# Attention with a mixture-of-experts step on one core: q, k and v loaded as one transfer of 128 partitions each

## The chip, the cores and the metric

One core of a Trainium2 chip. The metric is device time in microseconds of one execution of the whole program; what the host does before the launch (laying out arrays) is not in it.

## The reference

q, k and v have 8 batches, 8 heads, 576 positions and 64 columns of float32. Per batch and head: q and k are rotated by position, the scores are `q_rot @ k_rot.T / 8`, a softmax follows over the keys, and the result is `attn @ v`. The heads of a batch are put beside each other into x (8, 576, 512). Then, per batch:

```python
scores = np.einsum('bsd,d->bs', x, w_gate)
top_idx = np.argpartition(-scores[b], capacity)[:capacity]   # capacity = 128
xe = x[b, top_idx]
ye = np.maximum(xe @ w1, 0.0) @ w2                           # 512 -> 1024 -> 512
g = 1.0 / (1.0 + np.exp(-scores[b, top_idx]))
out[b, top_idx] = x[b, top_idx] + g[:, None] * ye
```

## The kernel before

The work goes in 32 **pairs** of heads (`n_pairs = B * NP`, four to a batch). Of a pair, 512 of the 576 positions lie as 128 partitions with 4 positions each, the other 64 apart. A pair passes these steps:

- **load** (line 388): k into `k_in`, q into `q_in`, v into `vt`, two buffers each, for the pair after next. k takes 2 transfers, q 3 and v 6, all issued on SyncE's queue (SP) by `dma` (L398). `vt` holds v twice, in partitions 0 to 63 and again in 64 to 127; this comes from a broadcast in the transfer: the source has a leading dimension of 2 with a step of zero.
- **rotate** (L434): on GpSimd, for pair 0 on VectorE; scratch tile `m`. **turn_qk** (L496 to L520): TensorE transposes, and ScalarE, VectorE and GpSimd split the result into a high and a low part (kh, kl, qh, ql).
- **attend**: nine units of 128 queries by 576 keys. Units 0 to 7 go in twos on the halves of TensorE (L588), unit 8 alone; VectorE finds each row's maximum (L605), ScalarE makes exponentials into `pab` (L609), and VectorE transposes these in blocks of 32 into `pt` (L623). Units 0 to 3 go into `pt0`, called c = 0, units 4 to 8 into `pt1`, c = 1. There is one buffer of each.
- **move** (L636): the 32-wide blocks have to change partitions, which is done by six transfers from SBUF to SBUF per c, on SP's queue too. Four can go at once, the last two wait for the first two:

```python
gone = [part(g, 2, g + 1, 0, turns) for g in (0, 2)]
for i, g in enumerate((0, 2)):
    part(g + 1, 2, g + 1, 1, turns)
for i, g in enumerate((0, 2)):
    part(g + 1, 0, g, 1, turns + [gone[i]])
```

- **value** (L665): 36 matmuls of TensorE per c (72 instructions in the profile), pt against v; for c = 0 they are all 64x128, for c = 1 some are 64x192. Copies to `ot` (L298, L300), transposes and gate scores (L709, L710), and rows times the softmax's reciprocals into `x` (L720) follow; each half batch is stored by two transfers (L772, L774).
- **route** and **experts** (L792 to L969), once per batch, are spread between the pairs that follow. w1 and w2 are loaded once, early (L995).

The order on each engine is not that of the code. Every step is recorded as an `Op` with engines, a key (a due time), the operations that it waits for and two durations: how long it holds its engine, and when its result is there. `Order.run` places them all by list scheduling and then emits them in that order. For transfers these pairs of numbers are constants: `LOAD, STORE = {"SP": (500, 2900)}, {"SP": (650, 4000)}` and `(700, 3300)` for a move. A transfer's size doesn't enter.

Of the kernel before, what the change touches and what calls it, by code (L numbers as in the profile page):

```python
# [227 lines left out]
def attention_moe_kernel(ctx: ExitStack, tc: tile.TileContext, q, k, v, w_gate, w1, w2, rope, outs, cap):  # L228
# [159 lines left out]
    def load(pi, names="kqv", after=()):  # L388
        b, j = divmod(pi, NP)
        key = at(pi, 0) - KEY["load"]  # L390
        main = lambda src: src[b, 2 * j:2 * j + 2, 0:512, :].rearrange("h (p t) d -> p h t d", t=NT)
# [5 lines left out]
        def dma(n, dst, src, use, late):  # L397
            o = op(LOAD, lambda: nc.sync.dma_start(dst, src), key + late, use.before + list(after))  # L398
            use.by(o)
            got[n].append(o)  # L400

        for n, src, use, late in (("k", k, kin, 0), ("q", q, qin, 1)):
            if n not in names:
                continue
            dst = use.tile
            dma(n, dst[:, 0:2 * NT, :].rearrange("p (h t) d -> p h t d", h=2), main(src), use, late)
            if n == "k":
                dma(n, dst[0:REM, 2 * NT:NS, :], src[b, 2 * j:2 * j + 2, 512:S, :].rearrange("h p d -> p h d"), use, late)
            else:
# [568 lines left out]
    def weights():  # L978
# [7 lines left out]
        for h in range(2):  # L986
            const_ready.append(op(LOAD, lambda h=h: nc.sync.dma_start(
                wg[64 * h:64 * h + 64, :, h], w_gate.rearrange("(j h d) -> h d j", h=2, d=D)[h]),
                at(0, 0.1), anchors[-1:]))
# [63 lines left out]

# [21 lines left out]
```

## Time and profile before

| | |
|---|---|
| median of 3 runs | 1051.77 us (1051.35 to 1051.9) |
| the profiled execution | 1053.8 us; span from its first to its last instruction 1052.1 us |
| mean granted TensorE clock | 0.803 of full speed |
| busy share: TensorE, VectorE, ScalarE, GpSimd | 60%, 52%, 34%, 40% |
| SP's DMA queue (q1) | 83104 packets, 115.12 MB, 41.7% of 16 DMA engines |

The span is what the profile's rows are cut from; the profiled execution's own time is 1.7 us longer. No engine is busy for much more than half of it, so what the engines wait for has to be read from the waits, by group of instructions, and then in one pair. A name such as `ps<-pt,vt` says that tile ps was written from pt and vt. "PEld" is TensorE's loading of weights. In a line of waits, `<-` names what ended the wait. SP issues transfers; a row "SPq" shows how long its queue was taken by the issue, not how long the transfer ran.

### The profile page before, as it was taken

What the parts mean: (1) busy time and instruction counts of PE and PEld (TensorE: products, weight loads), DVE (VectorE), ACT (ScalarE), POOL (GpSimd) and SP (SyncE); (2) the same over time, 40 slices, a digit from 0 to 9 for tenths busy, and PEclk for the clock granted to TensorE, in tenths of its full rate; (3) what the DMA queues carried; (4) which work ended last, traced back from release to release, by engine and by line L of the source; (5) the groups of instructions that cost most, each with busy time, mean ns of one, the idle gap of its engine ahead of it and who ended that gap; (6) DMA issues with size and microseconds to landing.
All of it is one profiled execution on the core that took longest, in us unless ns stands there. A gap on an engine that the chain in (4) does not pass through costs nothing.

```text
span 1052.1 us, 20374 instructions
## 1 busy us (share of the span) xinstructions
PE 628.9 (60%) x7696; PEld 533.8 (51%) x7696; DVE 544.1 (52%) x1342; ACT 362.6 (34%) x967; POOL 422.7 (40%) x491
## 2 busy tenths in 40 slices
PE   5436544576555555766456874555765475676677
PEld 3325534465454444655345764444655464565565
DVE  7245333675445545545457553446553465664452
ACT  3235333453323334423234432323442333442221
POOL 2649355745424175144270534440643262500011
PEclk9977766787778888878778886778887788887899
DMA  3643655434553443445343354543345354234520
GB/s 93 161 117 110 173 147 133 104 96 131 127 144 99 131 115 88 127 106 148 101 120 96 89 164 102 148 116 101 99 110 147 91 137 113 75 93 104 131 86 31
DMA packets 84626, 121.11 MB, mean 115 GB/s; under 512 B 27056, under 2 KB 69040, under 8 KB 84528
## 3 DMA queue, kind: packets, MB, share of 16 engines
q1 hardware_dynamic: 83104, 115.12, 41.7%
q0 software_dynamic: 1280, 4.20, 1.3%
q8 instruction: 61, 1.00, 0.4%
q10 hardware_dynamic: 144, 0.49, 0.1%
q14 instruction: 37, 0.30, 0.1%
HBM read 44.53 MB, written 11.53 MB: 53 GB/s over the span
## 4 chain that ended last, share of the span: by engine, by line
PE 35%; DMA 22%; SPq 19%; DVE 8%; issue 6%; POOL 5%; ACT 4%; POOLq 0%; ACTq 0%; DVEq 0%
PE ps L665 20%; DMA pt<-pt 18%; SPq L398 12%; PE ps L588 6%; SPq L636 6%; DVE pt L623 4%; PE ps L930 3%; ACT pab L609 3%; DVE nm L605 3%; PE ps L709 2%; PE ps L496 2%; DMA k_in<-k_dram 2%; POOL m L434 1%; PE ps L710 1%; DMA vt<-v_dram 1%
## 5 line engine op out<-in xcount | busy, mean ns | idle before, releaser
L665 PE MATMUL ps<-pt,vt 64*64 64x128 f32 (+1 forms) x4608 | 244.5, 359 | 341.2 <-DMA pt<-pt 287.3
L665 PEld LDWEIGHTS ps<-pt,vt 64*64 64x64 f32 x4608 | 215.8, 176 | 364.9 <-issue 350.5
L623 DVE STREAM_TRANSPOSE pt<-pab 128x576 f32<-128x576 f32 x256 | 185.0, 752 | 358.8 <-PE ps L665 329.9
L609 ACT ACTIVATE pab<-ps,nm 128x576 f32<-128x576 f32 x256 | 187.5, 740 | 130.7 <-DVE nm L605 130.6
L605 DVE TENSOR_REDUCE nm<-ps 128x1 f32<-128x576 f32 x288 | 200.8, 733 | 25.1 <-PE ps L588 23.6
L298 ACT COPY ot<-ps 64x64 f32<-64x64 f32 (+1 forms) x124 | 32.2, 287 | 400.3 <-PE ps L665 399.3
L434 POOL TENSOR_TENSOR rk<-k_in,m 128x512 f32<-128x512 f32 (+1 forms) x62 | 52.7, 867 | 175.6 <-PE ps L496 175.0
L588 PE MATMUL ps<-kh,qh 64*128 64x288 f32 (+1 forms) x576 | 96.3, 359 | 17.2 <-ACT pab L609 9.3
L511 POOL TENSOR_TENSOR kl<-xf,kh 128x512 fp32r<-128x512 f32 x31 | 39.4, 1270 | 161.4 <-ACT xf L509 161.2
L588 PEld LDWEIGHTS ps<-kh,qh 64*128 64x128 f32 (+1 forms) x576 | 57.5, 201 | 46.6 <-issue 20.7
L588 PE MATMUL ps<-kh,ql 64*128 64x288 f32 (+1 forms) x576 | 75.8, 306 | 5.6 <-POOL ql L511 5.6
L588 PE MATMUL ps<-kl,qh 64*128 64x288 f32 (+1 forms) x576 | 76.1, 305 | 0.0
L434 POOL TENSOR_TENSOR rq<-q_in,m 64x64 f32<-64x64 f32 (+1 forms) x93 | 57.4, 632 | 43.6 <-PE ps L496 30.8
L434 POOL TENSOR_TENSOR m<-k_in,tabs 128x320 f32<-128x320 f32 x62 | 52.3, 860 | 36.4 <-DMA k_in<-k_dram 34.8
L709 PE MATMUL ps<-ident,ot 128*128 128x128 f32 x160 | 47.7, 311 | 26.5 <-ACT pab L609 25.1
L588 PEld LDWEIGHTS ps<-kh,ql 64*128 64x128 f32 (+1 forms) x576 | 58.1, 198 | 6.7 <-POOL ql L511 6.6
L588 PEld LDWEIGHTS ps<-kl,qh 64*128 64x128 f32 (+1 forms) x576 | 59.1, 199 | 0.0
L609 ACT ACTIVATION_READ_ACCUMULATOR pab<-ps,nm 128x1 f32 x256 | 51.2, 200 | 0.0
L930 PE MATMUL ps<-w,xt 128*128 128x512 f32 x192 | 51.2, 406 | 0.0
L930 PE MATMUL ps<-w,ht 128*128 128x512 f32 x192 | 51.1, 405 | 0.0
L710 PEld LDWEIGHTS ps<-wg,ot 128*128 128x128 f32 x320 | 49.7, 211 | 0.9
L511 POOL TENSOR_TENSOR ql<-xf,qh 128x512 fp32r<-128x512 f32 x31 | 39.4, 1270 | 26.0 <-ACT xf L509 26.0
(105 smaller groups left out, 860.1 us busy)
## 6 DMA issues: line engine op xcount, KB each, us to landing
pt<-pt SPq DMA_DIRECT2D x192, 180.0 KB
pt<-pt SPq DMA_DIRECT2D x192, 144.0 KB
vt<-v_dram SPq DMA_DIRECT2D x128, 128.0 KB
k_in<-k_dram SPq DMA_DIRECT2D x32, 256.0 KB
q_in<-q_dram SPq DMA_DIRECT2D x32, 256.0 KB
out_dram<-x SPq DMA_DIRECT2D x16, 512.0 KB
vt<-v_dram SPq DMA_DIRECT2D x64, 32.0 KB
xe<-w_dram SPq DMA_DIRECT2D x8, 256.0 KB
```

Of the source, the lines that this page charges most:

```text
L398: o = op(LOAD, lambda: nc.sync.dma_start(dst, src), key + late, use.before + list(after))
L434: lambda: e.tensor_tensor(out, in0, in1, op=alu), key, after)
L511: d = op({"POOL": pool(n)}, lambda: nc.gpsimd.tensor_tensor(lo, xf.tile, hi.bitcast(F32), op=ALU.subtract), key, [c, y] + lu.before)
L588: nc.tensor.matmul(bank_of(bs[i])[:, n, 0:HALF], lt, rt, start=first, stop=last)
L605: lambda: nc.vector.tensor_reduce(nm.tile[:, u:u + 1], bank_of(b)[:, :, 0:HALF], axis=AX.XY, op=ALU.max, negate=True),
L609: lambda: nc.scalar.activation(dst.rearrange("p (n c) -> p n c", n=2), bank_of(b)[:, :, 0:HALF], AF.Exp, bias=nm.tile[:, u:u + 1], scale=1 ...
L623: lambda: nc.vector.transpose(pt[c].tile[:, 0:2, :, to, :].rearrange("p w m j -> p m w j"), src.rearrange("p (m w j) -> p m w j", w=2, j=32)),
L636: lambda: nc.sync.dma_start(flat[32 * to:32 * to + 32, w_to], flat[32 * at_:32 * at_ + 32, w_at]),
L665: nc.tensor.matmul(bank_of(acc)[64 * h:64 * h + 64, g, :].rearrange("p (w c) -> p w c", w=2)[:, :, c0:c0 + n], vt.tile[gp_, h, m % 2 * NT ...
L709: nc.tensor.transpose(bank_of(b)[:, i * P:i * P + P], cols, ident)
L710: nc.tensor.matmul(bank_of(b)[:, 400 + 2 * i:402 + 2 * i], cols, wg[:, j, :], start=True, stop=True)
L930: nc.tensor.matmul(bank_of(bank), lhs.tile[:, a, c * P:c * P + P], w[w_][:, c, fs], start=(c == 0 and i == 0), stop=(c == n - 1 and i == 2))
```

## The change

k, q and v come from the host in the layout that they have in SBUF, and each pair's load of each is one transfer with 128 rows: 640, 576 and 1152 elements a row. The host fills the rows that k leaves out of its last two blocks with zeros (which replaces a memset of `k_in`), writes v twice, and lays out the gate's vector in the same manner (two transfers and a memset become one transfer). `Order.run` gets a second clock for SP, `moving`: a transfer's data take 3.6 ns per KB, one after the other, and the result is there a constant time after that. The constants of loads, stores and moves change with it. The size of all three loads is given as 320.

```diff
+    PER_KB = 3.6
...
+                    if e == "SP":
+                        moving = max(moving, begin + takes) + self.PER_KB * o.size
+                        begin += max(0.0, moving - begin - takes)
...
-                    free[e] = begin + takes
+                    free[e] = t + takes if e == "SP" else begin + takes
...
-    LOAD, STORE = {"SP": (500, 2900)}, {"SP": (650, 4000)}
+    LOAD, STORE = {"SP": (500, 2000)}, {"SP": (600, 2000)}
...
-    for t_ in k_ins.tiles:
-        nc.gpsimd.memset(t_[REM:P, 2 * NT:NS, :], 0.0)
...
-    nc.vector.memset(wg, 0.0)
...
-        if "v" in names:
-            for h in range(2):
-                head = v[b, 2 * j + h]
-                for r in range(2):
-                    dma("v", vt.tile[:, h, NT * r:NT * r + NT, :].rearrange("p t d -> p (t d)"),
-                        head[256 * r:256 * r + 256].rearrange("(j t) d -> j (t d)", t=NT).unsqueeze(0).to_broadcast([2, 64, NT * D]),
-                        vt, 2)
-                dma("v", vt.tile[:, h, 2 * NT, :], head[512:S].unsqueeze(0).to_broadcast([2, 64, D]), vt, 2)
+        for i, (n, src, use) in enumerate((("k", k, kin), ("q", q, qin), ("v", v, vt))):
+            if n in names:
+                o = op(LOAD, lambda src=src, use=use: nc.sync.dma_start(use.tile, src[b, j]), key + i,
+                       use.before + list(after), size=320)
+                use.by(o)
+                got[n].append(o)
...
-                o = op({"SP": (700, 3300)},
+                o = op({"SP": (620, 2000)},
...
-                       key, needs)
+                       key, needs, size=144 + 36 * c)
...
+def _values(v):
+    B, H, S, D = v.shape
+    heads = v.reshape(B, H // 2, 2, S, D)
+    main = heads[:, :, :, 0:512].reshape(B, H // 2, 2, 2, 64, 4, D).transpose(0, 1, 4, 2, 3, 5, 6)
+    main = main.reshape(B, H // 2, 64, 2, 8, D)
+    once = np.concatenate([main, heads[:, :, :, 512:, None].transpose(0, 1, 3, 2, 4, 5)], 4)
+    return np.concatenate([once, once], 2)
```

The whole order on all engines is made anew from these numbers. Line numbers move with the edit (L398 becomes L397, L588 L569, L636 L617, L665 L646). Three places show it. First SP's queue in pair 11 (the second buffers of k and q, the first of v; pt00 is c = 0, pt10 is c = 1), from the moves of c = 1 of the pair before on; before:

```order
L636 DMA pt10_97<-pt10_97 32x1440 x6
L398 DMA k_in1_77<-k_dram 128x2x256
L398 DMA k_in1_77<-k_dram 64x2x64
L636 DMA pt00_96<-pt00_96 32x1152 x4
L398 DMA q_in1_75<-q_dram 128x2x256
L398 DMA vt0_89<-v_dram 128x1x256 x2
L398 DMA vt0_89<-v_dram 128x1x64
L398 DMA vt0_89<-v_dram 128x1x256 x2
L398 DMA vt0_89<-v_dram 128x1x64
L636 DMA pt00_96<-pt00_96 32x1152 x2
L398 DMA q_in1_75<-q_dram 64x64 x2
L636 DMA pt10_97<-pt10_97 32x1440 x6
```

and in the change:

```order
L617 DMA pt10_97<-pt10_97 32x1440 x4
L397 DMA k_in1_77<-k_dram 128x640
L617 DMA pt10_97<-pt10_97 32x1440 x2
L617 DMA pt00_96<-pt00_96 32x1152 x4
L397 DMA q_in1_75<-q_dram 128x576
L617 DMA pt00_96<-pt00_96 32x1152 x2
L397 DMA vt0_89<-v_dram 128x1152
L397 DMA k_in0_76<-k_dram 128x640
L617 DMA pt10_97<-pt10_97 32x1440 x6
```

The six issues of v stood between the fourth and the fifth move of c = 0; its one issue now stands behind the sixth, and the fifth has one q load ahead of it.

Second, TensorE in the same pair, around the value product of c = 0 (its last operand pt_96). Before:

```order
L588 MATMUL ps<-kh_81,qh_85 128x288 x4
L588 MATMUL ps<-kl_83,qh_85 128x288 x4
L588 MATMUL ps<-kh_81,ql_87 128x288 x4
L496 MATMUL ps<-ident,rk_79 128x128 x5
L496 MATMUL ps<-ident,rq_80 128x128 x5
L665 MATMUL ps<-pt_96,vt_90 64x2x64 x36
L588 MATMUL ps<-kh_81,qh_85 128x288 x4
```

and in the change:

```order
L849 LDWEIGHTS sel_121
L849 MATMUL ps<-tok_124,sel_121 128x5
L646 MATMUL ps<-pt_96,vt_90 64x2x64 x36
L569 MATMUL ps<-kh_81,qh_85 128x288 x2
L569 MATMUL ps<-kl_83,qh_85 128x288 x2
L569 MATMUL ps<-kh_81,ql_87 128x288 x2
L569 MATMUL ps<-kh_81,qh_85 128x288 x4
```

Twelve score products of the next pair (kh_81) and the transposes of its q stood ahead of the value product; it now comes before the first of them, behind small matmuls of the routing.

Third, SP's queue at the program's start; before:

```order
L398 DMA q_in0_74<-q_dram 128x2x256
L398 DMA q_in0_74<-q_dram 64x64 x2
L398 DMA vt0_89<-v_dram 128x1x256 x2
L398 DMA vt0_89<-v_dram 128x1x64
L398 DMA vt0_89<-v_dram 128x1x256 x2
L398 DMA vt0_89<-v_dram 128x1x64
L398 DMA k_in1_77<-k_dram 128x2x256
```

and in the change:

```order
L397 DMA k_in0_76<-k_dram 128x640
L397 DMA q_in0_74<-q_dram 128x576
L397 DMA vt0_89<-v_dram 128x1152
L397 DMA k_in1_77<-k_dram 128x640
L397 DMA q_in1_75<-q_dram 128x576
```

The sequence k, q, v, k of the next pair is the same; v of pair 0, which k of pair 1 follows, is one issue instead of six.

## Rows read from the trace of the kernel before

**Rows 1.** The page, the chain of work that ended last: shares of the span by engine and by line.

```profile
PE 35%; DMA 22%; SPq 19%; DVE 8%; issue 6%; POOL 5%; ACT 4%; POOLq 0%; ACTq 0%; DVEq 0%
PE ps L665 20%; DMA pt<-pt 18%; SPq L398 12%; PE ps L588 6%; SPq L636 6%; DVE pt L623 4%; PE ps L930 3%; ACT pab L609 3%; DVE nm L605 3%; PE ps L709 2%; PE ps L496 2%; DMA k_in<-k_dram 2%; POOL m L434 1%; PE ps L710 1%; DMA vt<-v_dram 1%
```

**Rows 2.** Groups of TensorE's instructions, shapes apart: line, engine, operation, tiles, shape, count | busy us, mean ns of one | idle us just before them, and what ended it.

```profile
L665 PE MATMUL ps<-pt,vt 64*64 64x128 f32 x3456 | 228.0, 368 | 334.3 <-DMA pt<-pt 284.9 <-DMA out_dram<-x 24.4 <-DMA k_in<-k_dram 23.0
L665 PE MATMUL ps<-pt,vt 64*64 64x192 f32 x1152 | 106.2, 332 | 6.8 <-ACT pab L609 4.3 <-DMA pt<-pt 2.4
```

**Rows 3.** Timeline of TensorE from 360 us: start us, us, engine, line, operation, tiles, shape, count, and in brackets the idle time before it and what ended it.

```profile
360.88 4.51 PE L665 MATMUL ps<-pt,vt 64*64 64x128 f32 x72 [10.13 <-DMA pt<-pt]
...
380.51 0.71 PE L496 MATMUL ps<-ident,rq 128*128 128x128 f32 x5
392.39 4.23 PE L665 MATMUL ps<-pt,vt 64*64 64x128 f32 x72 [11.16 <-DMA pt<-pt]
```

**Rows 4.** Timeline of SP's queue in the same stretch: start us, us that the issues took, and what they issue.

```profile
370.71 2.46 SPq L636 DMA_DIRECT2D pt<-pt  x4
373.26 0.53 SPq L398 DMA_DIRECT2D q_in<-q_dram  x1
373.89 9.77 SPq L398 DMA_DIRECT2D vt<-v_dram  x6
383.71 4.06 SPq L636 DMA_DIRECT2D pt<-pt  x2
```

**Rows 5.** Busy time by stretch (us from the span's start): length, then PE, PEld, DVE, ACT, POOL busy us (instructions), the granted TensorE clock, the share of 16 DMA engines that was busy, GB/s.

```profile
44.40:46.50 2.10, 2.10 (x45) 2.10 (x43) 0.00 (x0) 0.00 (x0) 1.94 (x4) 1.00 0.86 240
49.00:51.50 2.50, 1.51 (x16) 1.28 (x13) 2.50 (x5) 1.92 (x5) 0.00 (x0) 1.00 0.67 162
360.88:365.40 4.52, 4.52 (x73) 4.07 (x74) 0.00 (x0) 0.00 (x0) 0.00 (x0) 0.50 0.56 157
376.00:378.00 2.00, 2.00 (x16) 1.74 (x15) 1.95 (x5) 1.55 (x4) 1.16 (x1) 1.00 0.11 37
378.00:380.00 2.00, 2.00 (x18) 1.38 (x17) 2.00 (x6) 0.00 (x0) 0.00 (x0) 1.00 0.13 48
384.00:386.00 2.00, 0.00 (x0) 0.00 (x0) 0.00 (x0) 0.38 (x1) 2.00 (x3) 0.99 0.14 47
```

**Rows 6.** The page: all DMA packets, and issues by tile with their count and the KB of each.

```profile
DMA packets 84626, 121.11 MB, mean 115 GB/s; under 512 B 27056, under 2 KB 69040, under 8 KB 84528
...
pt<-pt SPq DMA_DIRECT2D x192, 180.0 KB
pt<-pt SPq DMA_DIRECT2D x192, 144.0 KB
vt<-v_dram SPq DMA_DIRECT2D x128, 128.0 KB
...
out_dram<-x SPq DMA_DIRECT2D x16, 512.0 KB
vt<-v_dram SPq DMA_DIRECT2D x64, 32.0 KB
```

**Rows 7.** The last pair, for which no load is left to make: timelines of VectorE, SP's queue and TensorE, a stretch of 2 us as in rows 5, and one step of the chain of waits (start us, us, what).

```profile
1001.29 1.42 DVE L623 STREAM_TRANSPOSE pt<-pab 128x576 f32<-128x576 f32 x2
...
1002.78 5.00 SPq L636 DMA_DIRECT2D pt<-pt  x6
...
1003.39 2.20 PE L665 MATMUL ps<-pt,vt 64*64 64x128 f32 x72
1009.64 5.24 PE L665 MATMUL ps<-pt,vt 64*64 64x192 f32 x72 [2.37 <-DMA pt<-pt]
...
1002.00:1004.00 2.00, 2.00 (x30) 1.47 (x31) 1.64 (x6) 0.00 (x0) 0.00 (x0) 1.00 0.09 20
...
1005.55 3.96 DMA pt<-pt
```

**Rows 8.** Waits of the whole execution: who waited for what, us in total, times, longest.

```profile
ACT ot L298 <- PE ps L665: 399.3, 56, 16.1
DVE pt L623 <- PE ps L665: 329.9, 38, 15.8
```

**Rows 9.** Stretches as in rows 5: before the first value product, from the first to the last of c = 0, after that, and one wait.

```profile
0.00:42.67 42.67, 15.97 (x75) 11.62 (x75) 22.17 (x69) 12.77 (x32) 17.39 (x32) 1.00 0.38 102
42.67:1003.39 960.72, 576.27 (x7334) 493.25 (x7334) 505.85 (x1210) 342.24 (x918) 398.91 (x449) 0.79 0.45 118
1003.39:1052.10 48.71, 36.70 (x290) 28.96 (x289) 16.05 (x63) 7.63 (x17) 6.36 (x11) 0.96 0.21 63
381.20:392.30 11.10, 0.02 (x1) 0.00 (x0) 1.39 (x6) 3.18 (x9) 10.14 (x12) 0.71 0.50 141
```

**Rows 10.** Issues by tile on SP's queue: count, ns of one (least/median/most), first and last start us.

```profile
L995 SPq DMA_DIRECT2D xe<-w_dram x8: 334/524/583, 49.0 to 153.6; - x8
L398 SPq DMA_DIRECT2D k_in<-k_dram x64: 371/667/2802, 0.8 to 866.6; - x64
L398 SPq DMA_DIRECT2D q_in<-q_dram x96: 378/541/1630, 2.1 to 868.6; - x96
```

**Rows 11.** Timelines of the start: GpSimd, VectorE, TensorE.

```profile
1.44 0.34 POOL L353 MEMSET k_in<- 64x128 f32 x2
22.13 1.69 POOL L434 TENSOR_TENSOR m<-k_in,tabs 128x320 f32<-128x320 f32 x2 [19.08 <-DMA k_in<-k_dram]
...
0.89 0.07 DVE L358 MEMSET wg<- 128x8 f32 x1 [0.89 <-PEq L1059]
5.42 0.89 DVE L434 TENSOR_TENSOR m<-k_in,tabs 128x320 f32<-128x320 f32 x2 [1.98 <-DMA k_in<-k_dram]
17.37 0.46 DVE L434 TENSOR_TENSOR rq<-q_in,m 64x64 f32<-64x64 f32 x2
...
26.83 1.11 PE L496 MATMUL ps<-ident,rk 128*128 128x128 f32 x4 [3.44 <-POOL rk L434]
33.15 1.11 PE L496 MATMUL ps<-ident,rq 128*128 128x128 f32 x4 [5.20 <-POOL rq L434]
42.67 4.70 PE L665 MATMUL ps<-pt,vt 64*64 64x128 f32 x72 [7.98 <-DMA pt<-pt]
```

More of the change, by code (lines that the diff above doesn't have):

```diff
@@ L75, in run @@
         mode, shared = 0, 0.0
-        count, fetched = 0, 0.0
+        count, fetched, moving = 0, 0.0, 0.0
         waiting = {e: [] for e in names}
@@ L227, in attention_moe_kernel @@
 @with_exitstack
-def attention_moe_kernel(ctx: ExitStack, tc: tile.TileContext, q, k, v, w_gate, w1, w2, rope, outs, cap):
+def attention_moe_kernel(ctx: ExitStack, tc: tile.TileContext, q, k, v, gate, w1, w2, rope, outs, shape, cap):
     nc = tc.nc
-    B, H, S, D = q.shape
+    B, H, S, D = shape
     DM = H * D
@@ L390, in load @@
         key = at(pi, 0) - KEY["load"]
-        main = lambda src: src[b, 2 * j:2 * j + 2, 0:512, :].rearrange("h (p t) d -> p h t d", t=NT)
-        rem = lambda src, h: src[b, 2 * j + h, 512:S, :]
         if "k" in names:
@@ L395, in load @@
         kin, qin, vt, got = loaded[pi]
[L397 to L409, printed above, removed]
-                for h in range(2):
-                    dma(n, dst[64 * h:64 * h + 64, 2 * NT, :], rem(src, h), use, late)
-        if "v" in names:
-            for h in range(2):
-                head = v[b, 2 * j + h]
-                for r in range(2):
-                    dma("v", vt.tile[:, h, NT * r:NT * r + NT, :].rearrange("p t d -> p (t d)"),
-                        head[256 * r:256 * r + 256].rearrange("(j t) d -> j (t d)", t=NT).unsqueeze(0).to_broadcast([2, 64, NT * D]),
-                        vt, 2)
-                dma("v", vt.tile[:, h, 2 * NT, :], head[512:S].unsqueeze(0).to_broadcast([2, 64, D]), vt, 2)
+        for i, (n, src, use) in enumerate((("k", k, kin), ("q", q, qin), ("v", v, vt))):
[4 more added lines that the diff above has]
+                got[n].append(o)
     def rotate(pi):
@@ L772, in half_done @@
         s0 = op(STORE, lambda: nc.sync.dma_start(outs[b][0:512, cs].rearrange("(p t) m -> p t m", t=NT), x.tile[:, 0:4, :]),
-                key, made)
-        s1 = op(STORE, lambda: nc.sync.dma_start(outs[b][512:S, cs], x.tile[0:REM, 4, :]), key, made)
+                key, made, size=512)
+        s1 = op(STORE, lambda: nc.sync.dma_start(outs[b][512:S, cs], x.tile[0:REM, 4, :]), key, made, size=64)
         x.by(s0, s1)
@@ L985, in weights @@
         ] + [(w2[c * P:c * P + P, :], [t_[:, c] for t_ in w2s]) for c in range(NFC)]
[L986 to L989, printed above, removed]
+        const_ready.append(op(LOAD, lambda: nc.sync.dma_start(wg, gate), at(0, 0.1), anchors[-1:], size=4))
         yield
@@ L995, in weights @@
             l = op(LOAD, lambda src=src, stage=stage: nc.sync.dma_start(stage, src), key,
-                   st.before + [anchors[i % 4 - 5]])
+                   st.before + [anchors[i % 4 - 5]], size=256)
             c = op({"ACT": act(DM)}, lambda hi=hi, stage=stage: nc.scalar.copy(hi, stage), key + 3000, [l])
@@ L1051, in _rope_tables, with _packed, _gate_columns @@
     return np.ascontiguousarray(np.concatenate([main, main, last, last], 2))
+def _packed(x, apart):
+    import numpy as np
+    B, H, S, D = x.shape
+    pairs = x.reshape(B, H // 2, 2, S, D)
+    main = pairs[:, :, :, 0:512].reshape(B, H // 2, 2, P, 4, D).transpose(0, 1, 3, 2, 4, 5).reshape(B, H // 2, P, 8, D)
+    last = pairs[:, :, :, 512:]
+    if apart:
+        rest = np.zeros((B, H // 2, P, 2, D), x.dtype)
+        rest[:, :, 0:S - 512] = last.transpose(0, 1, 3, 2, 4)
+    else:
+        rest = last.reshape(B, H // 2, P, 1, D)
+    return np.concatenate([main, rest], 3)
+def _values(v):
+    import numpy as np
+    B, H, S, D = v.shape
[4 more added lines that the diff above has]
+    return np.concatenate([once, once], 2)
+def _gate_columns(w_gate, D):
+    import numpy as np
+    out = np.zeros((2, D, w_gate.shape[0] // (2 * D), 2), w_gate.dtype)
+    for h in range(2):
+        out[h, :, :, h] = w_gate.reshape(-1, 2, D)[:, h].T
+    return out.reshape(2 * D, -1, 2)
 def kernel(q, k, v, moe_w_gate, moe_w1, moe_w2, moe_capacity):
@@ L1061 @@
     arrays = {
-        "q": q, "k": k, "v": v, "w_gate": moe_w_gate, "w1": moe_w1, "w2": moe_w2, "rope": _rope_tables(S, D),
+        "q": _packed(q, False), "k": _packed(k, True), "v": _values(v), "gate": _gate_columns(moe_w_gate, D),
+        "w1": moe_w1, "w2": moe_w2, "rope": _rope_tables(S, D),
     }
@@ L1071 @@
         with tc.manual_schedule():
-            attention_moe_kernel(tc, *aps, outs, int(moe_capacity))
+            attention_moe_kernel(tc, *aps, outs, (B, H, S, D), int(moe_capacity))
     r = run_bass_kernel_spmd(nc, [{f"{n}_dram": a for n, a in arrays.items()}], core_ids=[0])
```

## The prediction, made before the changed kernel ran

> **What bounds the kernel now.** I read the chain of waits first: a fifth of it is the value product (L665), 18% the moves of pt from SBUF to SBUF, 12% the issue of loads on SP's queue (L398) [rows 1]. Groups by shape then show where the waiting sits: the value product of c = 0 (64x128) stood idle 334.3 us, the one of c = 1, which begins with the other shape (64x192), 6.8 us, over 32 pairs each [rows 2]. Both wait for six moves of the same kind, so the moves alone are not slow.
>
> One pair shows the difference. TensorE has nothing left to do at 381.2 and starts the product of c = 0 only at 392.39, after 11.16 us [rows 3]. Meanwhile SP has issued four of its six moves at 370.71, then one q load, then six v loads that take 9.77 us to issue, and only at 383.71 the last two moves [rows 4]. The issue of v is slow because its transfers are: while they run, the DMA engines are busy 0.11 to 0.14 of their time at 37 to 48 GB/s, which is two engines of 16; where wide transfers run, 0.86 and 240 GB/s are reached [rows 5]. So v (four transfers of 128 KB and two of 32 in each pair, 576 KB or 590,000 bytes [rows 6]) takes some 590/45 = 13 us, and the last two moves of c = 0 stand behind it. The trace shows this in 31 pairs of 32.
>
> Two things follow from the wait. The product after it runs at half clock: 4.51 and 4.23 us [rows 3] at a granted clock of 0.50 [rows 5], against 2.20 us for the same 72 matmuls in the last pair, where nothing was waited for and the clock was 1.00 [rows 7]. And the other engines stop with it, since the transposes into pt and the copies of its result need the product's end [rows 8]: in one wait VectorE worked 1.39 us of 11.10, though GpSimd worked 10.14 [rows 9].
>
> **Part by part.** I start from the profiled span, 1052.1 us; that execution took 1053.8 with what lies around it, the median of the runs is 1051.77. So a sum made on the span stands within 0.3 us of the median, and I give it as it is.
>
> *v as one transfer of 128 partitions.* One issue in place of six. The nearest rows for its issue are the weight loads, also one row for each of 128 partitions: median 0.52 us [rows 10]. Its 590,000 bytes at 240 GB/s take 2.5 us. In the pair above, the last two moves would follow the first four and q: 370.71 + 2.46 + 0.53, so at about 373.7 instead of 383.71, done by 374.9; with 3.96 us from issue to landing, the longest that the chain shows in the undisturbed last pair [rows 7], and 1.2 us for q's 288 KB, c = 0 is ready at 380.1, before 381.2. The wait goes whole: **-334.3** for all pairs, with what comes back counted below.
>
> *Clock.* 31 products from about 4.3 (the rows have 4.23 to 4.70 [rows 3, 11]) to 2.20 us: **-65**. Bounds: -71 (4.5 to 2.2), and -40 if a third of the pairs still wait long enough to lose the clock.
>
> *The start.* k of pair 1 is now behind v of pair 0: GpSimd waits 19.08 us for it and begins at 22.13, and TensorE waits 3.44 and 5.20 us for GpSimd's rk and rq [rows 11]. With v as one wide transfer, k of pair 1 lands after some 1500 KB at 240 GB/s, 6.4 us and a few more of latency; then GpSimd waits for the scratch tile m2, which VectorE uses in pair 0's rotation until 17.83 [rows 11]. It begins some 4.3 us earlier, and the order now puts pair 0's first value product ahead of the transposes that wait for rq: **-6**, bounds 0 and -12.
>
> *k and q as one transfer each.* 2 and 3 issues become 1 and 1, at medians of 0.67 and 0.54 us [rows 10] some 2 us of SP's queue per pair. SP was late only through v, so nothing more: 0. k grows from 288 to 320 KB, 1 MB in all or 4 us of a DMA that is busy half the time: 0, covered by 18 us of other work in each pair. If that cover were gone, 4.
>
> *Memsets of k_in and wg.* 0.34 us on GpSimd before it waits 19 us for k, and 0.07 on VectorE before it waits 1.98 [rows 11]: 0.
>
> *The order, made with bytes counted.* The table of loads and moves says 2000 ns and 3.6 ns for each KB where it said 2900 to 3300. Value products therefore stand nearer to their moves than before, as the two excerpts of the order show: in pair 11 the c = 0 product is now ahead of twelve score products that stood before it, and v stands behind the six moves of c = 0. What a move really needs: from the end of the last transpose, 1002.71, to the product that reads it, 1009.64, 6.9 us pass with no load in the way [rows 7]. The order counts some 6 for this. Also it counts v as 320 KB where 576 come: 1.1 us too little at 240 GB/s where v is in front. Below: 0.2 us per pair, what the c = 1 product waits now (6.8 over 32) [rows 2] with k and q loads among its moves. Above: 2.5 us for each of the two products, a whole v in front of both. I take 1.0 per pair, near the lower row, since most pairs have v behind c = 0's moves: **+31**, bounds +6 and +155.
>
> *No more rests for the others.* Between the first value product and the last lie 960.72 us, 31.0 per pair [rows 9]. Without waits and slow clock it is (960.72 - 326 - 65)/31 = 18.4. In it TensorE must be busy (576.27 - 65)/31 = 16.5, VectorE 505.85/31 = 16.3, GpSimd 398.91/31 = 12.9. Each fits, but GpSimd loses the waits in which it caught up. I take +0.4 per pair, **+12**, bounds 0 and +37.
>
> Sum: 1052.1 - 334.3 - 65 - 6 + 31 + 12 = 689.8, so **690 us**, or 19.8 per pair.
>
> **A rule against it.** The two engines of v left fourteen free, as the share of 0.13 shows [rows 5]. The Trainium skill (DMA: Bandwidth & Descriptors, Queues, rings and completion order) says that on each DMA engine descriptors are consumed in ring order; by it a wide v fills all sixteen rings, so moves behind it wait for all of it. That is the first rival, and it would make 814 of the sum. The row of c = 1, 0.2 us with loads among its moves, speaks against its full price.
>
> **Rivals.**
> 1. *A load in front of every product.* v before c = 0's last moves and the 576 KB of two output stores or k and q before those of c = 1, with products placed too near: 2.5 us for both, 155 instead of 31: 814; at one of the two, 736. For it: the order counts too few bytes for v. Against: v stands behind c = 0's moves in the pair shown, and the product waits late only where TensorE comes early. 20% for above 725.
> 2. *Nothing comes back.* The order's latencies hold and VectorE and TensorE pack tighter, as c = 1 does now: 1052.1 - 334.3 - 71 - 12 + 6 = 641. 16% for below 665.
> 3. *The transfers stay narrow, and slower.* If a transfer of whole rows ran on two engines as v does, 1184 KB of loads at 45 GB/s would be 26.9 us per pair on them, and an eighth of 1944 KB of moves and 288 KB of stores [rows 6] another 6.3: 33.2 us, over the 31.0 of now, so about 43 + 31 x 33.2 + 49 = 1121 with the stretches before the first and after the last c = 0 product as they are [rows 9]. It decides from some 25 us of loads per pair on. Against: weight loads of the same shape run in a stretch at 162 GB/s and 0.67 [rows 5]; for it only that no load of 4.6 KB rows is in the trace. 2% slower, 1% for no change. The Trainium skill (DMA: Bandwidth & Descriptors, Why a DMA increments its semaphore by 16 and not by 1) lets the slowest dimension set the engines, 16 for 128 partitions, which agrees with 0.13 for v's leading 2; by it this rival falls away.
>
> That the DMA engines become the bound is no case: 122 MB (121 now [rows 6], 1 more for k) at 240 GB/s are 509 us. That the change does not do what it says is excluded by the order, which has three loads per pair.
>
> **How the numbers follow.** 61% for 665 to 725, around 690; 16% below, 20% above, up to 814, 3% for rival 3. The range takes in rival 2's 641 and rival 1 where two thirds of its price come: 645 to 770. Faster 0.97, same 0.01, slower 0.02, where 0.2% (2 us) is what a measurement can tell.
>
> **What would show it.** L665 64x128 idle falls from 334.3 to under 60 us, with waits of 1 to 3 us; its 72 matmuls take 2.2 to 2.6; the clock is 1.0 nearly throughout; v's issue is near 0.5 us; the DMA rate never stays at 45 GB/s; periods near 20 us. If waits over 5 us stay before c = 0, or move to c = 1, rival 1 is right; if VectorE or GpSimd is what TensorE waits for, the 12 were too few.

## The result and the profile after

| | before | after |
|---|---|---|
| median of 4 runs each | 1051.56 us | 697.27 us (694.99 to 702.56) |
| the profiled execution | 1053.8 us, span 1052.1 | 699.43 us, span 697.7 |
| mean granted TensorE clock | 0.803 | 0.951 |

The ratio is 0.6642, 95% interval 0.6598 to 0.6687. The forecast was 690 us, its range 645 to 770; the median lies 7 us above the forecast. In the tables below, e7's median and ratio take in one run of 704.0 us at a mean granted clock of 0.819, while its other three lie at 681.18 to 689.13.

From the page of the kernel after: busy time by engine, the granted clock in 40 slices, all DMA packets, SP's queue, and the chain that ended last, by engine and by line.

```profile
PE 583.9 (84%) x7696; PEld 489.8 (70%) x7696; DVE 543.9 (78%) x1350; ACT 362.1 (52%) x958; POOL 424.5 (61%) x489
...
PEclk9998888999899999999999999999999999999999
...
DMA packets 45950, 122.12 MB, mean 175 GB/s; under 512 B 8864, under 2 KB 18080, under 8 KB 45856
...
q1 hardware_dynamic: 44432, 116.17, 61.0%
...
PE 34%; DVE 23%; DMA 17%; issue 9%; ACT 7%; POOL 6%; SPq 3%; POOLq 0%; DVEq 0%; ACTq 0%
PE ps L646 18%; DMA pt<-pt 14%; DVE pt L604 9%; DVE nm L586 8%; PE ps L569 6%; PE ps L911 5%; ACT pab L590 4%; SPq L617 2%; PE ps L477 2%; DVE junk L792 2%; PE ps L690 1%; POOL m L415 1%; DMA xe<-out_dram,idx 1%; PE ps L691 1%; POOL rq L415 1%
```

Beside [rows 1] and [rows 6]: nearly the same bytes in little more than half the packets, SP's queue down from 19% to 3% of the chain, and VectorE up from 8% to 23%. No engine is the bound: TensorE is busy 84%.

The value products in TensorE's groups, shapes apart, as in [rows 2]:

```profile
L646 PE MATMUL ps<-pt,vt 64*64 64x128 f32 x3456 | 183.2, 305 | 30.5 <-DMA pt<-pt 13.6 <-issue 11.9 <-ACT pab L590 2.3
L646 PE MATMUL ps<-pt,vt 64*64 64x192 f32 x1152 | 112.2, 338 | 11.9 <-ACT pab L590 6.5 <-DMA pt<-pt 3.6 <-DMA q_in<-q_dram 1.0
```

334.3 us of idle time have become 30.5; busy time in the same group fell by 44.8. A third of the group's matmuls are c = 1's. Of c = 0's own 32 products the timeline gives 28.9 us of idle time, and busy times of 4.32 us each in the mean before and 2.91 after. What TensorE waits for now, in us in total, times, longest:

```profile
PE ps L690 <- ACT pab L590: 19.0, 17, 1.7
PE ps L569 <- ACT pab L590: 17.7, 19, 4.4
PE ps L646 <- DMA pt<-pt: 17.2, 14, 2.8
PE ps L646 <- issue: 12.5, 8, 4.9
```

No group holds more than 19 us. The transfers, with KB of each and the median from issue to landing (this column was empty for them in [rows 6]), and the loads' issues on SP, in ns (least/median/most), as in [rows 10]:

```profile
pt<-pt SPq DMA_DIRECT2D x192, 180.0 KB, 3.7
pt<-pt SPq DMA_DIRECT2D x192, 144.0 KB, 3.7
vt<-v_dram SPq DMA_DIRECT2D x32, 576.0 KB, 5.3
```

```profile
L397 SPq DMA_DIRECT2D k_in<-k_dram x32: 328/412/1057, 0.8 to 564.5; - x32
L397 SPq DMA_DIRECT2D q_in<-q_dram x32: 328/463/580, 1.3 to 572.0; - x32
L397 SPq DMA_DIRECT2D vt<-v_dram x32: 328/460/1290, 1.7 to 621.8; - x32
```

v takes 0.46 us to issue and 5.3 to land, where its six issues alone took 9.77 [rows 4]. Two products of c = 0 in TensorE's timeline, one that waits and one that does not, with the first of all and GpSimd's first rotation (start us, us, what, and in brackets the idle time before it):

```profile
18.42 1.69 POOL L415 TENSOR_TENSOR m<-k_in,tabs 128x320 f32<-128x320 f32 x2 [15.85 <-DVE rq L415]
...
27.73 4.72 PE L646 MATMUL ps<-pt,vt 64*64 64x128 f32 x72 [2.77 <-DMA pt<-pt]
...
94.59 0.66 PE L477 MATMUL ps<-ident,rk 128*128 128x128 f32 x4 [1.28 <-POOL rk L415]
98.17 4.80 PE L646 MATMUL ps<-pt,vt 64*64 64x128 f32 x72 [2.92 <-issue]
...
212.27 2.20 PE L646 MATMUL ps<-pt,vt 64*64 64x128 f32 x72
```

SP's queue ahead of the product that waits:

```profile
90.42 2.27 SPq L617 DMA_DIRECT2D pt<-pt  x2
92.74 0.58 SPq L397 DMA_DIRECT2D vt<-v_dram  x1
93.42 1.14 SPq L617 DMA_DIRECT2D pt<-pt  x2
94.61 0.58 SPq L973 DMA_DIRECT2D xe<-w_dram  x1
95.24 0.49 SPq L397 DMA_DIRECT2D k_in<-k_dram  x1
```

And stretches as in [rows 5] and [rows 9]: three that cover the execution (up to the first product of c = 0, to the last, after it), then the product that waits, and four stretches for later.

```profile
0.00:27.73 27.73, 14.36 (x68) 10.48 (x69) 20.68 (x63) 11.41 (x28) 9.83 (x23) 1.00 0.51 160
27.73:646.96 619.23, 531.94 (x7329) 449.44 (x7329) 506.44 (x1222) 343.05 (x913) 408.26 (x456) 0.95 0.68 185
646.96:697.70 50.74, 37.57 (x301) 29.88 (x300) 16.81 (x67) 7.60 (x17) 6.39 (x11) 0.93 0.20 60
...
94.00:96.00 2.00, 0.66 (x4) 0.42 (x4) 1.21 (x5) 1.53 (x4) 1.82 (x3) 1.00 0.92 221
96.00:98.00 2.00, 0.00 (x0) 0.00 (x0) 1.87 (x5) 1.60 (x4) 2.00 (x3) 0.79 1.00 303
98.17:102.97 4.80, 4.76 (x74) 4.06 (x74) 0.00 (x0) 0.62 (x1) 3.58 (x4) 0.50 1.02 298
...
346.00:352.72 6.72, 4.75 (x48) 3.70 (x45) 6.36 (x21) 5.16 (x15) 5.06 (x8) 1.00 0.84 229
352.72:357.05 4.33, 4.17 (x74) 3.79 (x74) 1.04 (x2) 1.55 (x4) 4.30 (x4) 0.61 1.06 320
584.00:590.21 6.21, 4.09 (x40) 3.21 (x39) 5.85 (x20) 4.95 (x13) 5.21 (x8) 1.00 0.88 235
590.21:592.80 2.59, 2.59 (x74) 2.21 (x74) 0.91 (x2) 1.56 (x4) 2.56 (x3) 1.00 1.04 309
```

The wait before 98.17 is the old one in small: v stands between the fourth and the fifth move of c = 0, the last two moves are issued by 94.56, and the product starts 3.6 us later, while the DMA engines are busy 0.92 to 1.00 at 221 to 303 GB/s (with loads of weights and of k behind v). The profile names only "issue" for this wait; that it is the moves' landing follows from the view of those two issues, 4.7 us after 93.42 and 94.02:

```profile
DMA to landing us min/median/max: 4.7/4.7/4.8
```

Before, the same place cost 11.16 us at 47 GB/s.

Counted pair by pair in the timelines of SP and TensorE, this place of v is where the waits of c = 0 are. v stands among the six moves of c = 0 in 15 of the 32 pairs, and 23.8 of the 28.9 us of idle time are theirs. It stands ahead of the first move, with at most other loads and stores between, in 8 pairs: 3.5 us, of which 2.8 are the first product's. The other 9 have 1.7 us. A pair of the second kind, in SP's queue and in TensorE's timeline; the product has no idle time before it:

```profile
405.79 0.33 SPq L397 DMA_DIRECT2D vt<-v_dram  x1
406.17 2.46 SPq L617 DMA_DIRECT2D pt<-pt  x4
...
416.83 2.20 PE L646 MATMUL ps<-pt,vt 64*64 64x128 f32 x72
```

The span splits into three sums that can be read for every run: TensorE's busy time, the idle time before value products (both shapes), and TensorE's other idle time, which is the rest.

| us | span | busy | before value products | other idle |
|---|---|---|---|---|
| before | 1052.1 | 628.9 | 341.1 | 82.1 |
| after | 697.7 | 583.9 | 42.4 | 71.4 |
| difference | -354.4 | -45.0 | -298.7 | -10.7 |

### The profile page after: what moved, and what is told of

The parts are those of the page before. It is cut to its first block, busy times and chain, and to the rows that moved or that the text cites. A ratio compares the mean times of both kernels' runs of the same rounds, so it can differ in the third digit from the quotient of the medians.

```text
span 697.7 us, 19908 instructions
## 1 busy us (share of the span) xinstructions
PE 583.9 (84%) x7696; PEld 489.8 (70%) x7696; DVE 543.9 (78%) x1350; ACT 362.1 (52%) x958; POOL 424.5 (61%) x489
## 4 chain that ended last, share of the span: by engine, by line
PE 34%; DVE 23%; DMA 17%; issue 9%; ACT 7%; POOL 6%; SPq 3%; POOLq 0%; DVEq 0%; ACTq 0%
PE ps L646 18%; DMA pt<-pt 14%; DVE pt L604 9%; DVE nm L586 8%; PE ps L569 6%; PE ps L911 5%; ACT pab L590 4%; SPq L617 2%; PE ps L477 2%; DVE junk L792 2%; PE ps L690 1%; POOL m L415 1%; DMA xe<-out_dram,idx 1%; PE ps L691 1%; POOL rq L415 1%
## 5 line engine op out<-in xcount | busy, mean ns | idle before, releaser
L646 PE MATMUL ps<-pt,vt 64*64 64x128 f32 (+1 forms) x4608 | 205.4, 313 | 42.4 <-DMA pt<-pt 17.2
L646 PEld LDWEIGHTS ps<-pt,vt 64*64 64x64 f32 x4608 | 177.5, 147 | 63.8 <-issue 24.8
L569 PE MATMUL ps<-kh,qh 64*128 64x288 f32 (+1 forms) x576 | 94.7, 350 | 20.9 <-ACT pab L590 17.7
L569 PEld LDWEIGHTS ps<-kh,qh 64*128 64x128 f32 (+1 forms) x576 | 56.3, 193 | 51.6 <-ACT pab L590 25.6
L569 PE MATMUL ps<-kh,ql 64*128 64x288 f32 (+1 forms) x576 | 76.7, 305 | 2.9 <-POOL ql L492 2.9
L569 PE MATMUL ps<-kl,qh 64*128 64x288 f32 (+1 forms) x576 | 76.0, 303 | 0.0
L302 ACT COPY ot<-ps 64x64 f32<-64x64 f32 (+1 forms) x112 | 28.2, 281 | 91.1 <-PE ps L646 90.3
L690 PE MATMUL ps<-ident,ot 128*128 128x128 f32 x160 | 47.2, 307 | 19.6 <-ACT pab L590 19.0
L569 PEld LDWEIGHTS ps<-kh,ql 64*128 64x128 f32 (+1 forms) x576 | 58.6, 195 | 4.1 <-POOL ql L492 4.0
L569 PEld LDWEIGHTS ps<-kl,qh 64*128 64x128 f32 (+1 forms) x576 | 58.9, 196 | 0.0
L690 PEld LDWEIGHTS ps<-ident,ot 128*128 128x128 f32 x160 | 30.6, 191 | 28.0 <-ACT pab L590 23.0
```

What stands on the lines that cost most here:

```text
L302: nc.scalar.copy(out, in_)
L569: nc.tensor.matmul(bank_of(bs[i])[:, n, 0:HALF], lt, rt, start=first, stop=last)
L646: nc.tensor.matmul(bank_of(acc)[64 * h:64 * h + 64, g, :].rearrange("p (w c) -> p w c", w=2)[:, :, c0:c0 + n], vt.tile[gp_, h, m % 2 * NT ...
L690: nc.tensor.transpose(bank_of(b)[:, i * P:i * P + P], cols, ident)
```

## The experiments

The theory is that v cost the time by its width: transfers with a leading dimension of 2 run on two DMA engines of 16. Rivals are that the number of issues did it, or the new order, or the loads of k and q. A second question is what the remaining 42.4 us before value products are. All runs in one table, with the profiled execution's sums as above; the ratio is to the kernel before, timed on the same chip.

| | median us | ratio, 95% interval | span | busy | before value products | other idle |
|---|---|---|---|---|---|---|
| e1 v alone | 701.18 | 0.666 (0.662 to 0.670) | 702.2 | 585.5 | 45.2 | 71.5 |
| e2 k and q alone | 1046.18 | 0.995 (0.992 to 0.998) | 1041.5 | 633.8 | 328.2 | 79.5 |
| e3 order alone | 1051.34 | 0.9987 (0.9958 to 1.0015) | 1050.3 | 645.6 | 309.0 | 95.7 |
| e4 new loads, old numbers | 698.63 | 0.6646 (0.6613 to 0.6680) | 696.9 | 583.9 | 38.1 | 74.9 |
| e5 v one narrow issue | 1009.18 | 0.9592 (0.9544 to 0.9640) | 1007.4 | 630.3 | 298.7 | 78.4 |
| e6 v in two of 64 | 706.51 | 0.669 (0.664 to 0.674) | 706.7 | 585.2 | 51.7 | 69.8 |
| e10 more bytes behind v | 749.84 | 0.7141 (0.7085 to 0.7198) | 746.0 | 596.0 | 77.3 | 72.7 |
| e11 v of one head | 675.32 | 0.6441 (0.6406 to 0.6476) | 673.3 | 575.3 | 27.8 | 70.2 |
| e7 true sizes | 687.04 | 0.6523 (0.6466 to 0.6580) | 679.5 | 584.0 | 25.6 | 69.9 |
| e9 the change again | 700.41 | 0.6667 (0.6644 to 0.6690) | 702.0 | 586.0 | 44.2 | 71.8 |
| e12 true sizes again | 686.36 | 0.6526 (0.6495 to 0.6558) | 686.1 | 588.9 | 26.0 | 71.2 |
| e8 loads by ScalarE | 713.46 | 0.6825 (0.6776 to 0.6874) | 711.8 | 599.0 | 42.0 | 70.8 |

### e1: v alone

The kernel before, with only v changed (the host's layout, and):

```diff
+            dma("v", vt.tile, v[b, j], vt, 2)
```

> Kernel before with v alone as one transfer of 128 rows; k and q in their 2 and 3 transfers, the old numbers of the order. Width theory (the loss came from v's transfers running on two DMA engines): nearly the whole gain, 695 to 720 us. Theory of the number of issues (SP's queue was the bound): v takes away 5 of the 8 issues per pair that the change takes away, so 5/8 of 354 us, about 830. Order theory (the gain came from the new order): over 1000.

701.18 us: v alone brings the whole gain but for 4 us, which lies within the intervals. Waits before value products fall to 45.2 us with k and q in their five transfers and the old numbers for the order.

### e2: k and q alone

```diff
-            dma(n, dst[:, 0:2 * NT, :].rearrange("p (h t) d -> p h t d", h=2), main(src), use, late)
...
+            dma(n, use.tile, src[b, j], use, late)
```

> Kernel before with k and q alone as one transfer each; v in its six broadcast transfers, the old numbers of the order. Width theory: within 1% of before, 1041 to 1062, since SP is late only behind v. Number of issues: 3/8 of the gain, about 920.

0.995: three issues less for each pair bring 5 us (2 to 8 by the interval) while v is still narrow; 12.9 us less before value products, 4.9 more busy. Beside a wide v no part of it can be told from scatter (e1 against e4: 701.18 and 698.63).

### e5: v in one issue, and narrow

The change, and its order, but v comes from one copy through a leading dimension of 2 with a step of zero, as before, in a single issue:

```diff
+                    s_ = s_.rearrange("p h t d -> p (h t d)").unsqueeze(0).to_broadcast([2, 64, 2 * (NT + NT + 1) * D])
...
-    return np.concatenate([once, once], 2)
+    return once
```

> The changed kernel, same order, but v comes as one transfer whose source is stored once and broadcast with a leading dimension of 2: one issue, rows of 4.6 KB, two DMA engines. Width theory: the gain is lost, since 590,000 bytes at 45 GB/s stand 13 us in the queue of two engines ahead of the next moves: 950 to 1080. Number of issues, or size of the packets: stays near 697, at most 710.

1009.18 us. SP's queue around one v, then stretches of the same pair, columns as in [rows 5], then the group and the landing times:

```profile
384.94 0.59 SPq L401 DMA_DIRECT2D vt<-v_dram  x1
385.59 2.45 SPq L621 DMA_DIRECT2D pt<-pt  x4
```

```profile
392.00:394.00 2.00, 0.00 (x0) 0.00 (x0) 1.58 (x5) 1.87 (x5) 2.00 (x3) 1.00 0.14 55
396.00:398.00 2.00, 0.00 (x0) 0.00 (x0) 0.00 (x0) 0.00 (x0) 1.84 (x4) 0.50 0.14 55
```

```profile
L650 PE MATMUL ps<-pt,vt 64*64 64x128 f32 x3456 | 220.4, 352 | 241.7 <-DMA pt<-pt 172.3 <-issue 67.8 <-ACT pab L594 1.6
```

```profile
pt<-pt SPq DMA_DIRECT2D x192, 144.0 KB, 14.5
```

The issue is as short as in the change, 0.59 us, but the transfer runs at 0.14 of the DMA engines and 55 GB/s, and the moves of c = 0 need 14.5 us in the median to land in place of 3.7. It is the width: this kernel differs from the change only in that, and in v being stored once, which e6 shows not to matter. Nor is it the packets, whose number and sizes are nearly those of the change:

```profile
DMA packets 45502, 122.12 MB, mean 121 GB/s; under 512 B 8416, under 2 KB 17632, under 8 KB 45408
```

The number of issues explains at most the 43 us between this and the kernel before on the same chip, and the order and the loads of k and q differ there too.

### e4: the change's loads with the old numbers of the order

```diff
-    PER_KB = 3.6
+    PER_KB = 0.0
...
+    LOAD, STORE = {"SP": (500, 2900)}, {"SP": (650, 4000)}
...
+                o = op({"SP": (700, 3300)},
```

> The changed kernel's loads with the old numbers for the order (2900, 4000 and 3300 ns, no time per KB). Width theory: 690 to 715, the order is worth 2% at most either way. Order theory: over 750.

698.63 against 697.27 us: the new numbers, as they stand in the change, are worth nothing that can be measured. The two orders are not alike, though. Here v stands among the moves of c = 0 in 25 pairs, in the change in 15; and TensorE comes to the product (its start less its idle time) 4.4 us after the issue of the last move has ended, in the median over the pairs, in the change after 3.0. The one can offset the other.

### e3: the order's numbers alone

The kernel before, with `moving`, the change's constants and sizes, k, q and v in their 11 transfers:

```diff
+            many = {"k": 2, "q": 3, "v": 6}[n]
+            o = op(LOAD, lambda: nc.sync.dma_start(dst, src), key + late, use.before + list(after), size=320 / many)
```

> Kernel before with the new numbers of the order alone (2000 ns and 3.6 ns per KB, sizes of the pair's loads as in the change, split over its 2, 3 and 6 transfers); all transfers as before. Width theory: within 2% of before, 1031 to 1073, v still runs on two engines. Order theory: at least 50 us faster.

No difference. The groups show what such an order does while v is narrow:

```profile
L670 PE MATMUL ps<-pt,vt 64*64 64x128 f32 x3456 | 224.6, 355 | 217.9 <-DMA pt<-pt 200.7 <-DMA k_in<-k_dram 15.4 <-issue 1.6
L670 PE MATMUL ps<-pt,vt 64*64 64x192 f32 x1152 | 132.3, 378 | 91.1 <-DMA pt<-pt 75.1 <-DMA q_in<-q_dram 12.6 <-DVE nm L610 2.6
```

Waits of c = 0 fell by 116 us and those of c = 1 rose by 84; the rest came back as slower products and other idle time. The reading is that the slow transfer delays whichever moves stand behind it.

### e6: v stored once, in two transfers of 64 partitions

```diff
+                        for r in range(2):
+                            nc.sync.dma_start(use.tile[64 * r:64 * r + 64], src[b, j])
...
-    return np.concatenate([once, once], 2)
+    return once
```

> The changed kernel, same order, v stored once by the host and loaded by two transfers of 64 rows each in place of one of 128. Width theory: 64 rows spread over all 16 engines as 128 do, so 690 to 705. If one whole transfer of 128 rows is what matters: slower by over 20 us.

706.51 us, a little over what was expected, and its interval overlaps that of the change, so whether the second issue costs something stays undecided. The copy made by the host is at least not what brings the gain: 64 rows in each transfer do, too.

### e10: 480 KB more behind each v

What the 42.4 us are was open. If a load only costs where a move happens to stand behind it, more bytes should mostly hide; rival 1 says they cost.

```diff
+                    if n == "v":
+                        nc.sync.dma_start(spare, src[b, j].rearrange("p h t d -> p (h t d)")[:, 0:960])
```

> The changed kernel, same order, with 480 KB more loaded per pair, right behind v into a spare tile that nobody reads: 15.7 MB in all. First rival (a load in front of the moves is what the products wait for): 492,000 bytes at 240 GB/s are 2 us per pair, 50 to 65 us slower, 750 to 762. Theory that v stands behind the moves that matter, with slack after it: under 15 us slower, 697 to 712.

The ratio rises by 0.050, some 52 us for 15.7 MB, or 3.3 us for each MB; the groups:

```profile
L652 PE MATMUL ps<-pt,vt 64*64 64x128 f32 x3456 | 193.0, 321 | 63.7 <-DMA pt<-pt 27.7 <-issue 11.1 <-DMA out_dram<-x 8.2
L652 PE MATMUL ps<-pt,vt 64*64 64x192 f32 x1152 | 110.5, 334 | 13.6 <-ACT pab L596 7.4 <-DMA pt<-pt 4.9 <-issue 1.1
```

Against the profile of the change, 34.9 us more stand before value products and 12.1 are longer busy time of TensorE, at a mean clock of 0.923 for 0.951. 27.5 of the 34.9 are in the 15 pairs in which v stands among the moves of c = 0: 51.3 us of idle time where the change has 23.8. That the bytes hide fails as a theory; the mechanism of rival 1 is at work, most of it in those pairs. Each pair also has one issue more. e6 adds an issue and no bytes, and its ratio lies 0.005 above the change's, not clear of scatter; so up to some 5 us of the 52 may be the issue's.

### e11: half of v's bytes

The complement. It leaves v of each pair's second head out, and no issue is added.

```diff
+                    if n == "v":
+                        nc.sync.dma_start(use.tile[:, 0], src[b, j][:, 0])
```

> The change, with v of the second head of each pair left out (its half of the tile stays at zero), so 288 KB for each pair in place of 576, 9.2 MB less in all; the order is that of the change. Complement of the doubled load, which cost 52 us for 15.7 MB. If the load in front of the moves costs by its bytes in this range too (3.3 us for each MB): some 30 us less, 660 to 675 us, with the value products' idle time under 20 us. If the change stands just below the point from which bytes count, so that only more of them cost: 690 to 699 us, idle 35 to 45 us.

675.32 against 700.41 us for the change on the same chip (e9): 25 us for 9.4 MB, 2.7 us for each MB. It just misses the expected 675 and 20 us of waits (27.8 were left), but the other theory, 690 to 699, is out. So bytes cost over the whole range tried, at 2.7 to 3.3 us for each MB; at the 298 to 320 GB/s of the stretches shown above a MB takes 3.1 to 3.4 us. Not all of the price is waiting: before value products it is 2.2 us for each MB in e10 and 1.7 here (16.4 us against e9), and most of the rest is longer busy time of TensorE. Nor do all pairs pay it: in the 15 with v among the moves of c = 0 the idle time is 11.2 us here, 22.6 in e9 and 51.3 in e10; in the other 17 together 4.6, 6.3 and 11.8. A load's bytes are therefore not hidden where moves that are waited for stand behind it, though the DMA engines are busy only 0.68 of the time.

### e7, e9 and e12: the sizes as they are

The change gives 320 KB for all three loads; this gives 320, 288 and 576, and 4.2 ns for each KB of every transfer in place of 3.6.

```diff
-    PER_KB = 3.6
+    PER_KB = 4.2
...
-                       use.before + list(after), size=320)
+                       use.before + list(after), size={"k": 320, "q": 288, "v": 576}[n])
```

> The changed kernel with the true sizes in the order (k 320, q 288, v 576 KB) and 4.2 ns per KB in place of 3.6. If the +1.0 us per pair of my sum comes from v's bytes counted short: up to 20 us faster, 677 to 690. If the order's numbers no longer matter, as the run with the old numbers says: 690 to 705.

687.04 us, so near the change that both were run once more beside each other.

> The change itself, once more, on the chip on which the true sizes run, so that the two can be told apart: 695 to 700 us.

> The change with the sizes of the loads counted truly (k 320, q 288, v 576 KB, 4.2 ns for each KB), once more beside the change. If the order it makes is really the better one: 1.0 to 2.0 per cent under the change, 683 to 690 us. If the earlier difference was scatter: within 0.5 per cent of the change, 694 to 700 us.

686.36 against 700.41 us (the change lies 3 us above its first timing): 2.0% less, and the intervals of the two ratios, 0.6495 to 0.6558 and 0.6644 to 0.6690, lie apart. This beats both kernels. The groups of e12:

```profile
L646 PE MATMUL ps<-pt,vt 64*64 64x128 f32 x3456 | 175.8, 294 | 13.9 <-DMA pt<-pt 6.9 <-ACT pab L590 6.2 <-DMA k_in<-k_dram 0.3
L646 PE MATMUL ps<-pt,vt 64*64 64x192 f32 x1152 | 118.1, 352 | 12.1 <-ACT pab L590 6.6 <-DMA pt<-pt 2.9 <-ACT xt L886 0.8
```

The spans of e9 and e12 differ by 15.9 us: 18.2 less before value products, 2.9 more busy, 0.6 less of other idle time. v's place in SP's queue is hardly what changed, since it stands among the moves of c = 0 in 14 pairs, where e9 has 15. But TensorE comes to the product later, 5.4 us after the issue of the last move has ended (median over the pairs) where e9 has 3.0, and the pairs with v among the moves wait 4.8 us in all, where they waited 22.6. Whether the sizes or the 4.2 ns moved the products is not separated. The clock does not follow: products of c = 0 take 2.50 us in the mean, 2.83 in e9, yet the mean granted clock is 0.942 against 0.947.

### e8: the loads in a queue of their own

e7's numbers, but ScalarE issues q, k and v, so no move stands behind a load in a queue.

```diff
+                o = op({"ACT": (80, 3500)}, lambda src=src, use=use: nc.scalar.dma_start(use.tile, src[b, j]), key + i,
```

> The change with the three sizes counted truly, and the loads of q, k and v issued by ScalarE, so in a queue of their own, and no longer in SP's queue with the moves. The order is made anew. Theory of the place in the queue: a move waits since the loads stand before it in SP's queue; with the loads in another, the value products' idle time (25.6 us with the true sizes, 42.4 with the change) falls under 15 us and the time to 668 to 682 us. Theory of the bytes: loads and moves share the same 16 DMA engines, whichever queue they come from, so nothing is gained: idle of the value products 20 to 40 us, 683 to 697 us. Third way: 96 issues of about 0.4 us on ScalarE, some 38 us of its time, delay the exponentials: units' waits for ScalarE rise by over 15 us and the time is over 697 us.

713.46 us, slower than the change and 27 us slower than e12. That ScalarE was held up is not the reason: the waits of TensorE's three main groups for its exponentials (L690, L569, L646) are 44.9 us, 42.4 in e12. The waits before value products are 42.0 us again. ScalarE's issues of v, SP's of the moves in one such pair, and stretches of it:

```profile
266.77 0.33 ACTq L397 DMA_DIRECT2D vt<-v_dram  x1
```

```profile
266.99 6.85 SPq L617 DMA_DIRECT2D pt<-pt  x6
```

```profile
270.00:272.00 2.00, 2.00 (x20) 1.96 (x19) 2.00 (x4) 1.61 (x6) 1.44 (x3) 1.00 1.06 346
274.00:276.00 2.00, 0.00 (x0) 0.00 (x0) 1.96 (x8) 1.58 (x4) 2.00 (x3) 0.94 1.01 284
```

The moves run beside v and then q (issued at 270.84) from another queue, and an output store stands behind them (from 273.89), with the DMA engines at 1.01 to 1.06; the product waited until 276.06 for the moves. So a queue apart does not take the waits away. That the bytes in the shared engines make them is argued from this and from e10 and e11. The Trainium skill (DMA: Bandwidth & Descriptors, Queues, rings and completion order) has SP's and ScalarE's queues as rings on the same 16 engines, with a completion that lands only after every earlier write of that engine, from whichever queue; that 42.0 us remain with a queue apart, as many as the 42.4 of the change, agrees. One reservation: the order was made anew, and its count of bytes knows nothing of ScalarE's transfers, so where the 16 us above e12 come from is not separated.

## Why the prediction was right, and where its terms were off

**The cause** was right: v's width, shown by e1, e5 and e3 together. One step on the way is not borne out: v's issue was said to be slow because its transfers are. In e5 v is as narrow, its one issue takes 0.59 us, and the time goes into the landing of the moves instead.

**-334.3, and +31 for new waits.** Together -303.3 were foretold, -298.7 came: 42.4 us are left where 6.8 + 31 were expected. The size holds, and its reason in part. The text took a price near the lower row "since most pairs have v behind c = 0's moves". That was read from pair 11: in the run v stands among those moves in 15 pairs and ahead of them in 8, and the 15 have most of the waits, which grow and shrink there with v's bytes (e10, e11). That the order places products too near to their moves is not refuted by the 38.1 us that remain with the old numbers (e4), since v stands among the moves in more pairs there; and with products that come 2.4 us later after their moves the waits fall to 26.0 us (e12). The text had seen that v is counted as 320 KB, and priced it at 1.1 us where v is in front; e12 bears that out, as far as the sizes and not the 4.2 ns made its order.

**-65 for the clock** was the step that failed most: TensorE's busy time fell by 45.0. It assumed that all 31 products would run at full clock. Counted in TensorE's timeline, 22 take 2.19 to 2.59 us, but 10 of the 32 still take over 3, nine of them in the 15 pairs with v among the moves and the tenth the first of all; the mean is 2.91 where 2.20 was expected. The bound of -40 allowed for a third of the pairs, and that is what happened, but with waits far shorter than thought: the product at 352.72 began after 0.80 us of idle time and ran at 0.61.

**-6 for the start** was low, within its bounds. Without its own wait (7.98 us before, 2.77 after) the first product of c = 0 could begin at 34.69 before and at 24.96 now, 9.7 us earlier. GpSimd's rotation began at 18.42 where 22.13 less 4.3 was said, released by VectorE's use of the scratch tile as foretold.

**+12 for rests that are gone** was wrong in sign. TensorE's other idle time between the first and the last product was 960.72 - 576.27 - 330.8 = 53.7 us before (330.8 is the 341.1 of [rows 2] less the first product's 7.98 and the 2.37 of the last pair [rows 7]) and 619.23 - 531.94 - 37.4 = 49.9 after (42.4 less 2.77 and 2.26): TensorE's rests for the others did not grow when the waits went.

**k and q, bytes, memsets at 0.** For k and q the runs leave some 5 us (e2). For bytes the reason for the zero is in doubt: k's 1 MB was called covered by 18 us of other work in each pair, while e10 and e11 put 2.7 to 3.3 us on a MB of v, nearly the 4 that the text gave for a cover that is gone; for k's bytes alone no run shows it. That the DMA engines are no bound remains true, but no bound does not mean hidden.

**Sum.** The periods came out at 619.23/31 = 19.98 us for 19.8. The errors, +20 for the clock, -17 for start and rests taken together, +5 for waits, nearly cancelled: 697.7 for 689.8. The agreement is better than the terms.

**Rivals.** Rival 1's mechanism is real and its price was too high: 42.4 us of waits, where it had 6.8 + 155. The Trainium skill's rule of ring order that stood beside it (DMA: Bandwidth & Descriptors, Queues, rings and completion order) agrees in direction with e10's +52 us; e8 says that leaving the ring does not help. Rival 2 missed in that something came back. Rival 3 fell: with v's rows of 4.6 KB the DMA engines reach a share of 1.00 at 303 GB/s.

**What was to be seen.** The idle time of L646 64x128 is 30.5 us, under 60, and v's issue 0.46 us, near 0.5. The clock is 0.9 or more in 35 of 40 slices, but in single products it is half, as above.

## What to carry to other kernels

Where an engine waits for small transfers, look at what runs in front of them: a busy share of the DMA engines near 0.13 while someone waits was here a transfer on about two engines of 16, and a layout with a leading dimension of 128 (or two of 64) was worth more than fewer issues or another order. After that, look for the loads that stand among moves that someone waits for, and give the waiting product some distance from them: 2.7 to 3.3 us for each MB came back here though the engines were busy only 0.68 of the time, another queue did not hide them, and with products placed 2.4 us later half of the idle time of c = 0 was gone (e12: 13.4 for 28.9 us). Read a place in a queue over all rounds and not in one. An agreement of a sum proves no term of it: take busy time, waits at one place and other idle time apart and compare each.

## What the runs showed of the hardware that was not expected

- The granted clock halves after little idle time, and not always: the product at 352.72 (0.80 us idle before it, TensorE busy 4.75 of the 6.72 us ahead) ran at 0.61 and took 4.33 us; the one at 590.21 (0.93 us idle, busy 4.09 of 6.21) ran at 1.00 and took 2.59. What tells them apart stays open.
- At the start the clock's column says 1.00 while matmuls run at half pace: the first product of c = 0 took 4.72 us. The 4.70 of the first product before [rows 11] is as slow as those at a granted 0.50 [rows 3, 5], so the column seems to be no evidence there.
- The share of busy DMA engines goes to 1.06 in stretches where loads and moves run beside each other, at up to 346 GB/s (e8), so the 240 GB/s taken from [rows 5] is no ceiling.
